# First feed-forward of a fused attention and experts kernel: three PSUM banks for the second product, the sum read out ahead of the weights' conversion, and the first row's conversions two steps later

## The chip, the core and the metric

The kernel runs on one core of a Trainium2 chip. The metric is the device time of one execution in microseconds. Names of engines: PE is TensorE (matmuls; PEld its weight loads), DVE is VectorE, ACT is ScalarE, POOL is GpSimd, SP is SyncE, which issues DMAs. A PSUM bank holds 128 x 512 numbers in fp32, the result of one product here.

## The reference

Three parts stand one behind the other: attention within hash buckets (2 x 8 heads, 768 positions, head size 64), whose output is a matrix x of 1536 x 512; a feed-forward with a rational activation; and a feed-forward of eight experts with a balanced gate. The change touches the second part, and the third takes its output.

```python
def _moe_ref(x, w_in, w_out, a, b):
    h = x @ w_in                                   # x: 1536 x 512, w_in: 512 x 2048
    h2 = h * h
    h3 = h2 * h
    P = a[0] + a[1] * h + a[2] * h2 + a[3] * h3
    Q = 1.0 + np.abs(b[0]) * np.abs(h) + np.abs(b[1]) * h2
    g = P / (Q + 1e-06)
    return (g @ w_out).astype(np.float32)          # w_out: 2048 x 512

def _moe2_ref(x, w_gate, w1, w2):
    P = ...                                        # softmax of x @ w_gate, balanced over 8 rounds
    out = np.zeros((N, D), dtype=np.float32)
    for e in range(E):                             # 8 experts, 512 x 1024 and 1024 x 512 each
        h = np.maximum(x @ w1[e], 0.0)
        out += P[:, e:e + 1] * (h @ w2[e])
    return out
```

The weights `moe_w_in` and `moe_w_out` are given as float64; the kernel is handed their 64-bit patterns and makes fp32 of them on the chip.

## The kernel before

Everything is fp32, and each product is made of three matmuls in a shorter format: every operand is split into a high part (rounded) and a low part (the rest), and high x high, high x low and low x high are added up in PSUM. In the trace, attention takes the time up to about 291 us, the first feed-forward 291 to 616, the experts the rest.

**Steps of the first feed-forward.** The 2048 hidden columns are taken in four rows of 512 (`qf`, NQ = 4), the 1536 tokens in three tiles of 512 (`tt`), and each pair of these in four column blocks of 128 (QF = 4). So there are 4 x 3 x 4 = 48 steps, counted by s in the loop of L633 and after; six more steps at its end belong to the experts. In step s PE makes a first product (`gemm1`, L346, 12 matmuls into a bank `h`), and then, from s = 6 on, a second product (`gemm2_a`, L396, 12 matmuls): for the pair that lies six steps back (QF + ALAG) it multiplies the four activated blocks `gh`, `gl` with one block of 128 columns of w_out, into one PSUM bank. `sum_a` then takes that bank out: in the first row (qf = 0, steps 6 to 17) ACT copies it to `part` (L104), in the later rows DVE adds it to `part` (L407). In the last row (steps 42 to 53) `sum_a` goes on one step later with the split of the result, the operand of the experts' products: x2h on ACT (L104), x2l on DVE (L107, called in L414).

**The banks.** Two tiles of two banks each are in use: `acca`, whose banks take turns for the second product (`j % 2`), and `cvt`, of which the first half is scratch for the conversions and the second half isn't used.

**The activation of a step.** ACT makes three functions of h (L364 to 366), POOL one product (L367), DVE two operations (L368, L369); one step later ACT makes Ln and Exp (L372, L373), DVE three operations (L374 to 376), ACT the copy `gh` (L104) and POOL the rest `gl` (L101).

**The conversions.** While a row is worked on, the eight weight blocks of the next row (four of w_in, four of w_out) are converted, 24 in all. A conversion of one block is: ACT Abs (L165), POOL a limit (L166), DVE four operations on the bits (L176 to 179, with the scratch bank `cvt`), POOL an addition (L182), ACT the high part, POOL the low part. Where it starts is a table (`prep_at`): for w_in at the steps 3, 4, 9, 10 of a row, for w_out at 6, 7, 12, 13. So of any three steps from 3 on, two have a conversion. With the last POOL operations of a block goes the issue of the load of the next raw block (L158, queue of SP).

**What sets the order.** The loop writes the order of PE, ACT, DVE and POOL by hand (a manual schedule). Each of the functions above is a generator that is carried on by `go` piece by piece, and the order in which the loop calls them is the order on each engine. Waits between engines are put in by the framework.

## Time and profile before

| | |
|---|---|
| runs | 1665.7, 1665.38, 1664.59 us; median 1665.38 |
| profiled execution | 1664.14 us, span 1662.4 us |
| PE busy | 1591.3 us (96% of the span) |
| DVE busy | 736.7 us (44%) |
| ACT busy | 563.3 us (34%) |
| POOL busy | 657.3 us (40%) |
| second product of the first feed-forward (L396, acca<-gh) | 384 matmuls, 399 ns each, idle before them 28.9 us, of which 21.7 us end with L407 |
| sum of a bank (L407) | 36 operations, 680 ns each |

The profile shows one execution. A group of it is one line of the kernel on one engine with its tile; "idle before" is the time in which that engine did nothing ahead of these instructions, with the operation that ended it. The span is counted from the first to the last instruction on the core; the execution's own time has a little more at both ends. Operations on DVE overlap at their ends, so the distance from start to start is a little shorter than the duration of one. An idle engine costs time only if it is the one that sets the end.

### The profile page before, as it was taken

Reading aid. Unit: us, or ns where it says so; the run is one execution under the profiler, and the core shown is the slowest. Engines: PE = TensorE matmul, PEld = TensorE weight load, DVE = VectorE, ACT = ScalarE, POOL = GpSimd, SP = SyncE. Lnnn points to the kernel's source line nnn. Section 1 sums busy time; section 2 is a strip of 40 time slices with the busy share of each in tenths; the row PEclk is TensorE's granted clock in tenths of the full one; section 3 lists DMA queues with packets and bytes.
Section 4 is the critical chain, followed back from the end, with each engine's and each line's share of the span. In section 5 each row is a group of like instructions: output and inputs, shape, how many; then the busy total and the mean of one; then the engine's idle time right before and its main releaser. Section 6 shows DMA issues by size and latency. Waiting matters only on the chain.

```text
span 1662.4 us, 19660 instructions
## 1 busy us (share of the span) xinstructions
PE 1591.3 (96%) x7683; PEld 1317.5 (79%) x7683; DVE 736.7 (44%) x1314; ACT 563.3 (34%) x1025; POOL 657.3 (40%) x696
## 2 busy tenths in 40 slices
PE   6999999798888999999999999999999999999998
PEld 5888888576666787888888888888888888888887
DVE  7999999788888742311111111111111111111112
ACT  4887888787676731111111111111111111111110
POOL 7688775677667650150051051042033024015000
PEclk8999999999999999999999999999999999999999
DMA  5232220022111110020020011011012002001001
GB/s 166 80 91 75 73 67 14 26 64 64 51 51 52 38 51 13 14 76 13 1 76 26 0 64 38 1 51 51 1 37 65 0 26 76 1 13 38 1 26 51
DMA packets 49389, 71.67 MB, mean 43 GB/s; under 512 B 4369, under 2 KB 35089, under 8 KB 49297
## 3 DMA queue, kind: packets, MB, share of 16 engines
q1 hardware_dynamic: 49296, 70.42, 14.0%
q8 instruction: 60, 0.98, 0.2%
q14 instruction: 33, 0.26, 0.0%
HBM read 59.79 MB, written 3.15 MB: 38 GB/s over the span
## 4 chain that ended last, share of the span: by engine, by line
PE 74%; DVE 13%; ACT 4%; POOL 4%; issue 3%; DMA 0%; DVEq 0%; POOLq 0%
PE h L346 33%; PE acc L441 31%; PE acca L396 3%; PE av L315 2%; PE pt L300 2%; POOL e L286 1%; DVE tq L374 1%; DVE tu L376 1%; DVE tr L375 1%; DVE e L278 1%; DVE tu L368 1%; DVE ptl L107 1%; DVE cvt L178 1%; DVE cvt L176 1%; DVE part L407 1%
## 5 line engine op out<-in xcount | busy, mean ns | idle before, releaser
L346 PE MATMUL h<-x2h,wa 128*128 128x512 f32 x1536 | 504.7, 390 | 0.0
L427 DVE SCALAR_TENSOR_TENSOR gl<-h,gh 128x512 fp32r<-128x512 f32 x192 | 132.7, 691 | 797.4 <-ACT gh L426 797.4
L441 PE MATMUL acc<-wb,gh 128*128 128x512 f32 x1536 | 474.4, 389 | 0.0
L426 ACT ACTIVATE gh<-h 128x512 fp32r<-128x512 f32 x192 | 114.8, 598 | 894.3 <-PE h L346 894.3
L346 PEld LDWEIGHTS h<-x2h,wa 128*128 128x128 f32 x1536 | 288.5, 188 | 60.1
L441 PEld LDWEIGHTS acc<-wb,gh 128*128 128x128 f32 x1536 | 288.0, 188 | 60.0
L441 PE MATMUL acc<-wb,gl 128*128 128x512 f32 x768 | 298.8, 389 | 0.0
L346 PE MATMUL h<-x2l,wa 128*128 128x512 f32 x768 | 298.8, 389 | 0.0
L98 POOL TENSOR_SCALAR wa<-ra 128x512 fp32r<-128x512 f32 x64 | 40.3, 630 | 533.5 <-PE h L346 533.4
L441 PEld LDWEIGHTS acc<-wb,gl 128*128 128x128 f32 x768 | 144.1, 188 | 29.9
L346 PEld LDWEIGHTS h<-x2l,wa 128*128 128x128 f32 x768 | 144.0, 188 | 29.6
L396 PE MATMUL acca<-gh,wb 128*128 128x512 f32 x384 | 129.8, 399 | 28.9 <-DVE part L407 21.7
L346 PE MATMUL h<-xh,wa 128*128 128x512 f32 x384 | 127.2, 393 | 6.9 <-DVE tu L376 6.9
L396 PEld LDWEIGHTS acca<-gh,wb 128*128 128x128 f32 x384 | 72.2, 188 | 55.2 <-DVE part L407 26.5
L107 DVE TENSOR_TENSOR ptl<-pt,pth 128x512 fp32r<-128x512 f32 x144 | 94.3, 680 | 15.3 <-ACT pth L104 14.5
L286 POOL TENSOR_SCALAR e<-e,rs 128x768 f32<-128x768 f32 x96 | 90.2, 951 | 24.2 <-DVE rs L284 14.6
L279 ACT ACTIVATE e<-e,nm 128x768 f32<-128x768 f32 x96 | 89.8, 935 | 8.5 <-DVE e L278 7.7
L278 DVE TENSOR_SCALAR_CACHE_REDUCE e<-s 128x768 f32<-128x768 f32 x96 | 90.8, 947 | 2.0 <-PE s L271 1.7
L300 PE MATMUL pt<-idr,e 128*128 128x128 f32 x576 | 82.5, 278 | 9.2 <-DVE ptl L107 4.0
L346 PEld LDWEIGHTS h<-xh,wa 128*128 128x128 f32 x384 | 72.5, 189 | 23.6 <-DVE tu L376 8.6
L101 POOL TENSOR_TENSOR wa<-ra,wa 128x512 fp32r<-128x512 f32 x64 | 84.0, 1313 | 5.3
L101 POOL TENSOR_TENSOR wb<-rb,wb 128x512 fp32r<-128x512 f32 x64 | 83.7, 1308 | 5.2
(149 smaller groups left out, 2027.2 us busy)
## 6 DMA issues: line engine op xcount, KB each, us to landing
ra<-in_moe_w_dram SPq DMA_DIRECT2D x32, 512.0 KB
rb<-in_moe_w_dram SPq DMA_DIRECT2D x32, 512.0 KB
ra<-in_moe_w_in_dram SPq DMA_DIRECT2D x16, 512.0 KB
rb<-in_moe_w_out_dram SPq DMA_DIRECT2D x16, 512.0 KB
qkv<-in_q_dram SPq DMA_DIRECT2D x16, 192.0 KB
qkv<-in_k_dram SPq DMA_DIRECT2D x16, 192.0 KB
qkv<-in_v_dram SPq DMA_DIRECT2D x16, 192.0 KB
a<-a SPq DMA_DIRECT2D x16, 192.0 KB
```

The lines of the kernel that those rows point to most:

```text
L98: pool.tensor_scalar(hi, src, 1.0, 0.0, ALU.mult, ALU.add)
L101: pool.tensor_tensor(lo, src, hi.bitcast(F32), ALU.subtract)
L107: dve.tensor_tensor(lo, src, hi.bitcast(F32), ALU.subtract)
L278: dve.tensor_scalar(e[j], s[:, 0:S], BIG, None, ALU.min, ALU.min, accum_out=nm)
L279: act.activation(e[j], e[j], AF.Exp, bias=nm, scale=-1.0, accum_out=rs[:, j:j + 1])
L286: pool.tensor_scalar(e[j], e[j], rs[:, j:j + 1], 0.0, ALU.mult, ALU.add)
L300: pe.transpose(pt[:, c, j * P:(j + 1) * P], e[j][:, cc * P:(cc + 1) * P], idf)
L346: pe.matmul(hps, lhsT=a[:, c], rhs=x[:, c], start=m == 0, stop=m == 3 * KC - 1)
L396: pe.matmul(o, lhsT=l[:, js], rhs=r, start=m == 0, stop=m == 3 * QF - 1)
L426: act.activation(gh, hps, AF.Relu)
L427: dve.scalar_tensor_tensor(gl, hps, 0.0, gh.bitcast(F32), ALU.max, ALU.subtract)
L441: pe.matmul(o, lhsT=l[:, js], rhs=r, start=f == 0 and m == 0, stop=f == EF - 1 and m == 2)
```

## The change

Four things are changed.

- The second product goes to three banks in turn: step s writes bank s mod 3 (n * 4 + j is s - 6). The first two are the two halves of `acca`, the third is the second half of `cvt`, whose first half stays the scratch of the conversions.
- In a step, the sum of the second product (`sum_a`) is called ahead of the DVE operations of a conversion, not behind them.
- The second part of `sum_a` (x2h and x2l, last row) is called near the end of the step that follows, just ahead of that step's sum, not near its beginning.
- The table of the conversions: in the first row w_in starts at the steps 5, 6, 9, 10, not 3, 4, 9, 10, and w_out at 8, 11, 12, 13, not 6, 7, 12, 13. The other rows keep their steps.

```diff
@@ -170,7 +170,7 @@
 
 
         ci = c.bitcast(I32)
-        pc = c if cvt is None else cvt[:, 0]
+        pc = c if cvt is None else cvt
         pi = pc.bitcast(I32)
         low, high = bits[:, :, 0], bits[:, :, 1]
         dve.tensor_scalar(pi, ci, 5, 2, ALU.logical_shift_left, ALU.logical_shift_right)
@@ -386,7 +386,7 @@
 
     def gemm2_a(n, j):
         qf, tt = units[n]
-        o = acca[:, j % 2]
+        o = acca[(n * 4 + j) % 3]
         js = slice(j * P, (j + 1) * P)
         m = 0
         for f in range(QF):
@@ -399,7 +399,7 @@
     def sum_a(n, j):
 
         qf, tt = units[n]
-        o = acca[:, j % 2]
+        o = acca[(n * 4 + j) % 3]
         if qf == 0:
             part[tt, j] = sums.tile([P, 512], F32, tag=f"sum{tt}{j}", name="part")
             act_copy(part[tt, j], o)
@@ -596,6 +596,7 @@
     sums = ffn_pool("sums", 1)
 
     acca, cvt = two_banks("acca"), two_banks("cvt")
+    acca, cvt = (acca[:, 0], acca[:, 1], cvt[:, 1]), cvt[:, 0]
     NU, NS, NB_ = len(units), len(units) * QF, len(steps)
     QS = TT * QF
 
@@ -606,8 +607,8 @@
 
     for qf in range(NQ):
         for j in range(QF):
-            prep_at(qf * QS + (3, 4, 9, 10)[j], 0, (qf + 1) * QF + j)
-            prep_at(qf * QS + (6, 7, 12, 13)[j], 1, (qf + 1) * QF + j)
+            prep_at(qf * QS + ((3, 4) if qf else (5, 6))[j] if j < 2 else qf * QS + 7 + j, 0, (qf + 1) * QF + j)
+            prep_at(qf * QS + ((6, 7) if qf else (8, 11))[j] if j < 2 else qf * QS + 10 + j, 1, (qf + 1) * QF + j)
     for e in range(E):
         for f in range(EF):
             i = FF // P + e * EF + f
@@ -639,7 +640,6 @@
             old_w = narrowing
             narrowing = [prep_weights(m, i) for m, i in preps.get(s, ())]
             narrowing = [w for w in narrowing if go(w)]
-            old_s = [w for w in summing if go(w)]
             for w in old_w:
                 go(w)
             for w in acting:
@@ -652,13 +652,15 @@
                 go(w)
             for w in old_w:
                 go(w), go(w)
-            for w in narrowing:
+            old_s, summing = summing, []
+            for w in old_s:
                 go(w)
-            summing = []
             if 0 <= u < NU:
                 w = sum_a(u, j)
                 if go(w):
                     summing.append(w)
+            for w in narrowing:
+                go(w)
             acting = [new] if n < 0 else []
         assert not (summing and any(go(w) for w in summing)) and not narrowing
 
```

On DVE, a step of a later row that has a conversion, before (L374 to L376 and L368, L369 belong to the activation, L176 to L179 to the conversion, L407 is the sum):

```order
L375 SCALAR_TENSOR_TENSOR tr<-tu,na,tr 128x512
L376 SCALAR_TENSOR_TENSOR tu<-tq,tr 128x512
L368 TENSOR_TENSOR tu<-tu,h 128x512
L369 SCALAR_TENSOR_TENSOR tu<-tu,na,h 128x512
L176 TENSOR_SCALAR cvt<-c 128x512
L177 SCALAR_TENSOR_TENSOR ra<-ra,cvt 128x512
L178 TENSOR_SCALAR cvt<-ra 128x512
L179 SCALAR_TENSOR_TENSOR ra<-ra,cvt 128x512
L407 TENSOR_TENSOR part<-part,acca 128x512
L374 SCALAR_TENSOR_TENSOR tq<-tq,dbias,tr 128x512
```

and after:

```order
L375 SCALAR_TENSOR_TENSOR tr<-tu,na,tr 128x512
L376 SCALAR_TENSOR_TENSOR tu<-tq,tr 128x512
L368 TENSOR_TENSOR tu<-tu,h 128x512
L369 SCALAR_TENSOR_TENSOR tu<-tu,na,h 128x512
L407 TENSOR_TENSOR part<-part,acca 128x512
L176 TENSOR_SCALAR cvt<-c 128x512
L177 SCALAR_TENSOR_TENSOR ra<-ra,cvt 128x512
L178 TENSOR_SCALAR cvt<-ra 128x512
L179 SCALAR_TENSOR_TENSOR ra<-ra,cvt 128x512
L374 SCALAR_TENSOR_TENSOR tq<-tq,dbias,tr 128x512
```

The sum has moved from behind the four operations of the conversion to ahead of them.

On PE, the end of the first product (into `h`) and the beginning of the second product of step 23, with the waits that the program carries (the number behind an engine's name is that of its semaphore), before:

```order
L346 MATMUL h_5623<-xl_99,wa_4944 128x512
L346 MATMUL h_5623<-xh_96,wa_4944 128x512
L396 MATMUL acca_4157<-gh_5138,wb_4398 128x512 [waits DVE_49]
L396 MATMUL acca_4157<-gl_5139,wb_4398 128x512
L396 MATMUL acca_4157<-gh_5138,wb_4398 128x512
```

and after:

```order
L346 MATMUL h_5623<-xl_99,wa_4944 128x512
L346 MATMUL h_5623<-xh_96,wa_4944 128x512
L396 MATMUL cvt_4158<-gh_5138,wb_4490 128x512 [waits DVE_49]
L396 MATMUL cvt_4158<-gl_5139,wb_4490 128x512
L396 MATMUL cvt_4158<-gh_5138,wb_4490 128x512
```

The product writes the tile `cvt` in place of `acca`; there is one wait for DVE in both. The same place in the step behind it, 24, before:

```order
L346 MATMUL h_5673<-xl_99,wa_5215 128x512
L346 MATMUL h_5673<-xh_96,wa_5215 128x512
L396 MATMUL acca_4157<-gh_5349,wb_5054 128x512 [waits DVE_49,Activation_49]
L396 MATMUL acca_4157<-gl_5350,wb_5054 128x512 [waits Pool_49]
L396 MATMUL acca_4157<-gh_5349,wb_5054 128x512
```

and after:

```order
L346 MATMUL h_5673<-xl_99,wa_5215 128x512
L346 MATMUL h_5673<-xh_96,wa_5215 128x512
L396 MATMUL acca_4157<-gh_5349,wb_5054 128x512 [waits Activation_49]
L396 MATMUL acca_4157<-gl_5350,wb_5054 128x512 [waits Pool_49]
L396 MATMUL acca_4157<-gh_5349,wb_5054 128x512
```

Here, where the bank is the first of `acca`, the wait for DVE is gone and that for ACT, which makes `gh`, is left.

On DVE in the last row, from one sum to the next (the tile part_4482 of before is part_4461 of after), before:

```order
L407 TENSOR_TENSOR part_4482<-part_4482,acca_4157 128x512
L107 TENSOR_TENSOR x2l_6378<-part_4482,x2h_6377 128x512
L374 SCALAR_TENSOR_TENSOR tq_6389<-tq_6389,dbias_299,tr_6428 128x512
L375 SCALAR_TENSOR_TENSOR tr_6428<-tu_6387,na_297,tr_6428 128x512
L376 SCALAR_TENSOR_TENSOR tu_6387<-tq_6389,tr_6428 128x512
L368 TENSOR_TENSOR tu_6434<-tu_6434,h_6401 128x512
L369 SCALAR_TENSOR_TENSOR tu_6434<-tu_6434,na_297,h_6401 128x512
L407 TENSOR_TENSOR part_4533<-part_4533,acca_4157 128x512
```

and after:

```order
L407 TENSOR_TENSOR part_4461<-part_4461,acca_4157 128x512
L374 SCALAR_TENSOR_TENSOR tq_6385<-tq_6385,dbias_299,tr_6426 128x512
L375 SCALAR_TENSOR_TENSOR tr_6426<-tu_6383,na_297,tr_6426 128x512
L376 SCALAR_TENSOR_TENSOR tu_6383<-tq_6385,tr_6426 128x512
L368 TENSOR_TENSOR tu_6432<-tu_6432,h_6401 128x512
L369 SCALAR_TENSOR_TENSOR tu_6432<-tu_6432,na_297,h_6401 128x512
L107 TENSOR_TENSOR x2l_6395<-part_4461,x2h_6394 128x512
L407 TENSOR_TENSOR part_4511<-part_4511,cvt_4158 128x512
```

The x2l operation on a sum's result has moved from right behind that sum to just ahead of the next sum; its ACT copy x2h has moved in the same way, from ahead of the next Ln and Exp to behind the next gh.

## Rows read from the trace of the kernel before

**Rows 1.** Windows by stretch: us, busy us (instructions) of each engine, PEclk, DMA share, GB/s.

```profile
320.00:403.00 83.00, 73.96 (x313) 57.85 (x311) 70.87 (x106) 68.41 (x115) 62.22 (x56) 1.00 0.19 58
403.00:531.00 128.00, 109.43 (x466) 86.44 (x467) 114.37 (x172) 87.56 (x142) 87.90 (x78) 1.00 0.17 54
...
616.00:1650.00 1034.00, 1034.00 (x4571) 850.52 (x4570) 206.93 (x346) 116.17 (x195) 224.16 (x235) 1.00 0.10 30
```

**Rows 2.** Waits of PE: who waits for whom, us in total, times, longest.

```profile
PE acca L396 <- DVE part L407: 21.7, 18, 3.0
```

**Rows 3.** Timeline of PE, first matmuls of second products: start, us, what, [idle before <-releaser].

```profile
389.26 0.50 PE L396 MATMUL acca<-gh,wb 128*128 128x512 f32 x1 [0.68 <-ACT part L104]
...
411.02 0.50 PE L396 MATMUL acca<-gh,wb 128*128 128x512 f32 x1 [1.06 <-DVE part L407]
...
423.84 0.50 PE L396 MATMUL acca<-gh,wb 128*128 128x512 f32 x1 [1.64 <-DVE part L407]
...
430.64 0.50 PE L396 MATMUL acca<-gh,wb 128*128 128x512 f32 x1 [1.04 <-DVE part L407]
...
436.21 0.39 PE L396 MATMUL acca<-gh,wb 128*128 128x512 f32 x1
...
528.76 0.50 PE L396 MATMUL acca<-gh,wb 128*128 128x512 f32 x1 [1.07 <-DVE part L407]
```

**Rows 4.** Timeline of DVE, same stretch.

```profile
414.31 0.68 DVE L407 TENSOR_TENSOR part<-part,acca 128x512 f32<-128x512 f32 x1
...
423.11 0.68 DVE L407 TENSOR_TENSOR part<-part,acca 128x512 f32<-128x512 f32 x1
...
429.90 0.68 DVE L407 TENSOR_TENSOR part<-part,acca 128x512 f32<-128x512 f32 x1
...
433.92 0.68 DVE L407 TENSOR_TENSOR part<-part,acca 128x512 f32<-128x512 f32 x1
...
438.56 0.69 DVE L368 TENSOR_TENSOR tu<-tu,h 128x512 f32<-128x512 f32 x1 [0.75 <-ACT tu L366]
...
439.95 0.69 DVE L176 TENSOR_SCALAR cvt<-c 128x512 int32<-128x512 int32 x1
...
442.73 0.68 DVE L407 TENSOR_TENSOR part<-part,acca 128x512 f32<-128x512 f32 x1
...
449.53 0.68 DVE L407 TENSOR_TENSOR part<-part,acca 128x512 f32<-128x512 f32 x1
```

**Rows 5.** Timeline of DVE in the first row: its stall for ACT (first of four).

```profile
343.08 0.75 DVE L374 SCALAR_TENSOR_TENSOR tq<-tq,dbias,tr 128x512 f32<-128x512 f32 x1 [2.14 <-ACT tr L373]
```

**Rows 6.** Timeline of SP (a load of bits), and the window after its landing.

```profile
332.53 6.48 SPq L158 DMA_DIRECT2D rb<-in_moe_w_out_dram  x2
...
335.50:336.00 0.50, 0.50 (x4) 0.41 (x3) 0.50 (x1) 0.47 (x2) 0.50 (x1) 1.00 0.00 0
```

**Rows 7.** Timeline in the last row: PE, then DVE, then ACT, then DVE again.

```profile
561.55 0.49 PE L396 MATMUL acca<-gh,wb 128*128 128x512 f32 x1
...
591.66 0.39 PE L396 MATMUL acca<-gh,wb 128*128 128x512 f32 x1
...
572.95 0.68 DVE L407 TENSOR_TENSOR part<-part,acca 128x512 f32<-128x512 f32 x1
...
573.67 0.63 ACT L104 ACTIVATE x2h<-part 128x512 fp32r<-128x512 f32 x1 [1.34 <-DVE part L407]
...
579.03 0.68 DVE L407 TENSOR_TENSOR part<-part,acca 128x512 f32<-128x512 f32 x1
```

**Rows 8.** Timeline of PE after its two longest waits, and windows behind each.

```profile
315.84 0.50 PE L346 MATMUL h<-xh,wa 128*128 128x512 f32 x1 [3.15 <-DVE tu L376]
...
317.10:320.50 3.40, 3.40 (x10) 2.61 (x9) 3.30 (x6) 3.02 (x5) 2.45 (x3) 0.51 0.28 100
...
404.22 0.50 PE L396 MATMUL acca<-gh,wb 128*128 128x512 f32 x1 [3.01 <-DVE part L407]
...
404.20:410.00 5.80, 5.74 (x24) 4.43 (x24) 5.63 (x9) 2.32 (x5) 4.35 (x4) 1.00 0.26 90
```

## The prediction

> **What bounds the kernel now.** I read the busy time by stretch first, then the waits of TensorE (PE), then the rows of the first feed-forward one by one. By stretch [rows 1], PE is busy for the whole 1034.00 us from 616 to 1650, the second feed-forward: nothing the change does to other engines can gain there. From 320 to 403 PE is idle for 83.00 - 73.96 = 9.0 us and from 403 to 531 for 128.00 - 109.43 = 18.6 us; the reader should see that this first feed-forward is the only place where the edited lines run and PE waits. PE's largest wait of this kernel's second half is that of the second product for the sum L407: 21.7 us in 18 waits [rows 2].
>
> The rows show what that wait is. I number the steps of the first feed-forward s; the second product of step 22 starts at 423.84 and of 23 at 430.64, both just after a sum, and that of 24 at 436.21 without a wait [rows 3]. The product at 423.84 writes the bank whose own sum had started at 414.31, 9.5 us earlier; it started 0.73 us after the sum at 423.11, that of the other bank [rows 4]. So the wait goes by the tile, a pair of banks, and not by the bank. That fact decides most of this case.
>
> What bounds three steps is a loop through VectorE (DVE) and PE: sum 429.90 -> product 430.64 (0.74) -> product 436.21 (5.57) -> L368 at 438.56 (2.35) -> L176 at 439.95 (1.39) -> sum 442.73 (2.78: the four operations of a conversion) -> sum 449.53 (6.80) [rows 3, 4]. Together 19.63 us. Product 20 starts at 411.02 and product 38 at 528.76 [rows 3]: 117.74 us for six such periods, 19.62 each. Matmuls alone would want less: 4571 in 1034.00 us [rows 1] are 0.226 us each, 5.43 us for the 24 of a step, 16.3 us for three.
>
> **The change, part by part. Three banks and sums ahead of conversions, steps 20 to 38.** The third bank is half of the tile whose other half is scratch for the conversions. If waits go by the tile there as well, the product into bank 0 waits for no sum, that into bank 1 for the sum of the step before, which now stands ahead of the conversion, and that into bank 2 (every third step: 20, 23, ... 38) for the last operation of the step before's conversion, since that writes or reads the same tile. Behind the waiting matmul on PE stands the rest of its product and the next step's first product, whose h ScalarE (ACT) needs next, and DVE behind it. So the new loop is: last operation of the conversion to the product 0.75, to the next product 5.57, to L368 2.35, L368 and L369 1.39, sum 0.60, conversion 2.78, then the five activation operations 3.42 (two sums without a conversion between them start 433.92 - 429.90 = 4.02 apart, less 0.60 for the sum), sum 0.60, and 2.18 up to the start of the conversion's last operation (2.78 less 0.60) [rows 4]. The sum is 19.64 us against 19.63. The loop has the same instructions in another order: **0 gained**. What does change is the shape: two waits of 1.64 and 1.04 us [rows 3] become one of about 3.0.
>
> **The first row, up to step 20.** Here the sums are ACT copies and DVE sets the pace: a step with a conversion takes it 3.42 + 2.78 = 6.20 us, one without stalls 2.14 us for ACT [rows 5], so 5.56. The change moves two conversions of each matrix by two to four steps, but leaves as many steps of each kind, so the pace to product 17 stays (389.26 before [rows 3]). At steps 8 and 11 the conversion now also waits for an ACT copy out of bank 2, with L374 of the next step queued behind it on DVE; nearest is DVE's stall of 2.14 for ACT [rows 5], of which I take 0.3 to 0.4 us each, since the copy is a short one that starts earlier: **+0.7**. From product 17 to 20 it took 411.02 - 389.26 = 21.76 us before, because the first sums stood behind conversions; by the new loop it takes 19.6: **-2.2**. Together **-1.4**; bounds 0 (the copies cost what a full stall of 2.14 costs, less the 2.2) and -3 (both hidden). Each moved conversion also moves its ACT and GpSimd operations, and the next load of raw bits on SyncE's queue behind them. That load is issued at 332.53 and by 335.50 nothing moves any more [rows 6]: 3.0 us, where it is wanted a step (5.4 us) or more later. I cost it at 0; without that cover it would be under 1 us of ACT's wait, once.
>
> **The last row's x2h and x2l, steps 44 to 49.** Before, the copy to x2h stands ahead of Ln and Exp on ACT and waits for the sum: sum 572.95, copy 573.67 after a wait of 1.34, next sum at 579.03 [rows 7], 6.08 us for a step in which the matmuls want 5.43. Five steps took 591.66 - 561.55 = 30.11 us [rows 7] against 5 x 5.43 = 27.2. After the change the copy follows gh a step later, when its sum is long done, and x2l stands behind L369; the loop opens and PE is next late for nothing: **-2.9**; bounds -1.5 (half the loop stays through the x2l operation ahead of the sum, some 0.7 us on DVE in each of four steps) and -3.
>
> **The clock.** What the merged waits do to PE's clock is not free. After the wait of 3.15 us before 315.84 the granted clock is 0.51 in 317.10:320.50, that is 1.2 in place of 2.4 GHz, after PE had idled; after the wait of 3.01 us before 404.22 it stays at 1.00 [rows 8]. One drop loses 3.40 x 0.49 = 1.7 us of matmul time. It counts as far as it falls in the 7.9 us (5.57 + 2.35) in which the loop goes through PE; I take 1.4, between 0.9 and 1.7. The waits of about 3 us after the change are nine: before products 11 and 14 and the seven from 20 to 38. (That before product 7, where DVE is late anyway, hides its drop as 317.10 does now.) Of the two nearest rows one dropped, so half of nine: five drops x 1.4 = **+7.0**.
> By the Trainium skill, page "TensorE: Matmul & The Clock Gate", section "HAM oscillation — how this bites in real kernels", waits between batches of matmuls put the clock down again each time, so that every batch pays; the wait before 315.84 agrees, that before 404.22 doesn't. By that rule all nine drop, which is the second rival.
>
> **Sum.** -1.4 + 0 - 2.9 + 7.0 = +2.7 us. The profiled execution took 1664.14 us (its span 1662.4), so 1666.8; it lies 1.2 us under the median of the runs, 1665.38, and on the median the forecast is **1668.1 us**.
>
> **The rivals.** (1) The clock stays up: the merged waits behave like that before 404.22, none or one drops. Then -4.3 to -2.9: 1661.1 to 1662.5. For it: of PE's 18 waits for sums none is followed by a drop. Against it: none but one of those was as long, and that at 315.84, as long, was. (2) Slower: the wait for the conversion puts the clock down nearly every time. The place is each bank-2 product, the price 1.4 us, and it decides from six drops: -4.3 + 6 x 1.4 = +4.1, 1669.5; all nine give +8.3, 1673.7; at 1.7 each, 1676. I take 1671 as its middle. (3) The third bank works as three free banks would: the product waits for its own bank's sum alone, two steps back. Then the loop falls to DVE's work, 3 x 4.02 + 2 x 2.78 = 17.6 us, which is still above PE's 16.3: -2.0 in each of six periods, -12, with no wait long enough for a drop: 1665.4 - 4.3 - 12 = 1649. The rows at 414.31 and 423.84 speak against it, unless the two halves of the scratch tile are told apart.
> By the Trainium skill, page "PSUM — Partial Sum Buffer", section "PSUM bank collisions raise a hardware error", a guard by bank is what the chip needs, so waits by bank would do; the trace shows them by the pair.
>
> **How the numbers follow.** Two to five drops (1663.9 to 1668.1, forecast at the upper end, where half of nine puts it): 0.41. None or one, 1661 to 1662.5: 0.20. Six or more, 1669.5 and up: 0.36. Free banks, 1649: 0.03. A difference of 0.2%, 3.3 us, is about what a measurement of this kernel can tell from none. Faster by more than that (under 1662.1) holds free banks and nearly all of the first rival, 0.22; slower (over 1668.7) the second rival and a little of the forecast's spread, 0.38; within, 0.40. The range leaves out free banks, the lowest of the first rival (the -3 bounds without a drop) and the top of the second (eight or more drops): 1660.5 to 1672.5.
>
> **What would show it.** In the trace after, product 20 should start near 409.6, product 38 near 527.4 plus some 1.4 us for each drop there, the periods being 19.6 us or that plus a drop; the bank-2 products should wait about 3.0 us and be released by L179, no other product for DVE; the tail should run at 5.4 us a step without waits. Stretches of half clock, about 3.4 us long, should follow four to six of the waits. Bank-2 products released by a sum, or periods near 17.6, would make me wrong by 12 us; more waits in the tail, or drops after all waits or none, by 3 to 6.

## The result

The changed kernel takes 1683.96 us (median; 1682.86 to 1684.93) against 1664.99 us for the kernel before in the same runs: a ratio of 1.0114, 95% interval 1.0096 to 1.0131. It is 19 us slower; the forecast was 1668.1, the range ended at 1672.5.

The profiled execution took 1682.86 us, span 1681.1 us against 1662.4. First the stretches of the kernel after, in the columns of [rows 1] (us, busy us of PE, PEld, DVE, ACT, POOL with instructions, PEclk, DMA share, GB/s):

```profile
320.00:403.00 83.00, 69.32 (x273) 55.41 (x273) 67.28 (x100) 62.68 (x105) 59.01 (x54) 0.90 0.21 64
403.00:531.00 128.00, 109.87 (x426) 87.96 (x425) 104.59 (x157) 81.49 (x132) 80.01 (x73) 0.89 0.16 50
531.00:561.00 30.00, 27.00 (x107) 21.74 (x106) 22.65 (x35) 17.44 (x28) 19.14 (x18) 0.89 0.12 36
...
636.00:1660.00 1024.00, 1024.00 (x4526) 842.89 (x4525) 204.11 (x343) 114.55 (x193) 223.01 (x233) 1.00 0.10 30
```

In 128 us from 403 PE is busy for as long as before (109.87 against 109.43 us) and does fewer matmuls in it (426 against 466): the loss isn't in more waiting but in slower matmuls. PEclk tells it: 0.89 and 0.90, where [rows 1] had 1.00.

The waits of PE, as in [rows 2]:

```profile
PE cvt L396 <- DVE rb L179: 16.1, 5, 4.0
PE cvt L396 <- DVE ra L179: 14.7, 5, 3.8
...
PE acca L396 <- ACT part L104: 4.0, 1, 4.0
...
PE acca L396 <- DVE part L407: 0.3, 1, 0.3
```

The 18 waits for sums have become one, and in their place stand ten for L179, the last operation of a conversion, all of them of products into `cvt`: the third bank waits by the tile, as forecast. The products that answer to [rows 3] and [rows 7], here 11, 14, 20, 23, 26, 38, 44 and 49 in the order of time:

```profile
353.82 0.50 PE L396 MATMUL cvt<-gh,wb 128*128 128x512 f32 x1 [3.81 <-DVE ra L179]
...
376.05 0.79 PE L396 MATMUL cvt<-gh,wb 128*128 128x512 f32 x1 [4.01 <-DVE rb L179]
...
416.91 0.77 PE L396 MATMUL cvt<-gh,wb 128*128 128x512 f32 x1 [3.10 <-DVE rb L179]
...
439.26 0.50 PE L396 MATMUL cvt<-gh,wb 128*128 128x512 f32 x1 [3.01 <-DVE ra L179]
...
460.49 0.80 PE L396 MATMUL cvt<-gh,wb 128*128 128x512 f32 x1 [3.01 <-DVE rb L179]
...
546.43 0.79 PE L396 MATMUL cvt<-gh,wb 128*128 128x512 f32 x1 [3.00 <-DVE rb L179]
...
582.02 0.39 PE L396 MATMUL cvt<-gh,wb 128*128 128x512 f32 x1
...
609.96 0.50 PE L396 MATMUL acca<-gh,wb 128*128 128x512 f32 x1 [0.33 <-DVE part L407]
```

Some of the first matmuls behind a wait last 0.8 us and not 0.5: they run at half clock. Windows behind products 20, 23 and 26 of the kernel after, with the full-speed stretch between the first two:

```profile
416.00:422.70 6.70, 5.79 (x14) 4.58 (x15) 4.38 (x8) 3.29 (x6) 5.37 (x5) 0.50 0.25 78
422.80:439.80 17.00, 13.99 (x61) 11.26 (x61) 14.24 (x23) 10.70 (x17) 8.48 (x8) 1.00 0.10 31
439.90:443.20 3.30, 3.30 (x9) 2.57 (x8) 2.66 (x4) 1.92 (x4) 2.87 (x3) 0.50 0.48 138
460.40:463.70 3.30, 3.21 (x8) 2.54 (x9) 3.23 (x6) 1.19 (x3) 2.76 (x3) 0.50 0.31 87
```

So goes every wait of 3 us or more in this trace: with each of the nine that were forecast (3.8 and 4.0 us long in the first row, 3.0 to 3.1 later), and with the 4.0 us ahead of product 7, PE's clock goes to 0.50 for 3.4 or 6.8 us. The tenth wait for L179, 1.82 us ahead of product 17, has no such stretch. The rows give this account of the 18.7 us of span (18.3 of them; the other 0.4 come after product 49):

| stretch | before, us | after, us | moved | forecast |
|---|---|---|---|---|
| start to product 20 | 411.02 | 416.91 | +5.9 | -1.4 and its drops |
| product 20 to 38, six periods | 117.74 | 129.52 | +11.8 | 0 and its drops |
| product 38 to 44 | 32.79 | 35.59 | +2.8 | the drop behind product 38 |
| product 44 to 49 | 30.11 | 27.94 | -2.2 | -2.9 |

### The profile page after: what moved, and what is told of

The parts are those of the page before. It is cut to its first block, busy times and chain, and to the rows that moved or that the text cites. A ratio compares the mean times of both kernels' runs of the same rounds, so it can differ in the third digit from the quotient of the medians.

```text
span 1681.1 us, 19668 instructions
## 1 busy us (share of the span) xinstructions
PE 1606.3 (96%) x7683; PEld 1333.7 (79%) x7683; DVE 738.8 (44%) x1314; ACT 562.7 (33%) x1025; POOL 656.8 (39%) x696
## 4 chain that ended last, share of the span: by engine, by line
PE 79%; DVE 9%; POOL 4%; ACT 4%; issue 2%; DMA 0%; DVEq 0%; SPq 0%; POOLq 0%
PE h L346 35%; PE acc L441 31%; PE cvt L396 3%; PE acca L396 3%; PE av L315 2%; PE pt L300 2%; POOL e L286 1%; DVE e L278 1%; DVE ptl L107 1%; DVE tq L374 1%; DVE tu L376 1%; DVE tr L375 1%; PE s L270 1%; PE s L271 1%; ACT tq L365 1%
## 5 line engine op out<-in xcount | busy, mean ns | idle before, releaser
L396 PE MATMUL acca<-gh,wb 128*128 128x512 f32 x256 | 86.1, 398 | 4.4 <-ACT part L104 4.0
L396 PE MATMUL cvt<-gh,wb 128*128 128x512 f32 x128 | 56.7, 511 | 30.8 <-DVE rb L179 16.1
```

Of the source, the lines that this page charges most:

```text
L396: pe.matmul(o, lhsT=l[:, js], rhs=r, start=m == 0, stop=m == 3 * QF - 1)
```

## The experiments

The runs of four kernels each stood beside runs of the kernel before; every difference below is from the kernel before in the same runs (medians 1664.43, 1664.42 and 1665.23 us) unless another kernel is named, ratios with their 95% intervals. A start read from a trace belongs to one execution. The feed-forward doesn't begin at the same time in each: PE's first wait for L376 ends at 300.88 in the trace of the kernel before and between 299.87 and 302.46 in those of the others. So starts compared across kernels carry 1 to 1.5 us of that; lengths within one trace don't.

**The waits filled.** The half clock is to be taken away and the waits' end left as it is: PE gets work where it would wait. `fill` (its definition is left out here) is twelve matmuls of the step's wa and xh into a bank of its own (`dm`) that nobody reads. Product 8 gets one too, though it doesn't wait in the changed kernel.

```diff
+            if s in (7, 8, 11, 14) or s % 3 == 2 and 20 <= s <= 38:
+                fill(*divmod(s, QF))
             if 0 <= u < NU:
                 gemm2_a(u, j)
```

> The changed kernel with twelve extra matmuls (a repeat of high x high of the first product, into a bank that nobody reads) ahead of the second products of steps 7, 8, 11, 14 and 20, 23 to 38, where PE waits 3 to 4 us for the conversion. The DVE chain that ends the wait is left as it is. Theory A, the clock: the 19 us are lost in the stretches of half clock behind these waits (ten stretches, together 51 us long, in the changed kernel's trace). With 2.7 us of the wait filled the granted clock stays at 1.00, the six periods from product 20 to 38 go from 21.1 to 22.4 us to 19.6, and the time comes to 1660 to 1664 us, 20 us under the changed kernel. Theory B, the waits themselves or the later conversions of the first row set the end and the low clock only follows: the periods stay above 21 us and the time at 1682 or above.

Measured: 1668.27 us, 1.0023 (1.0014 to 1.0033) of before: 15 to 16 us less than the changed kernel, with more work. The clock is 1.00 in the whole feed-forward; the products 20 and 38 (L396 is L403 in this file) and the two windows:

```profile
413.98 0.47 PE L403 MATMUL cvt<-gh,wb 128*128 128x512 f32 x1 [0.38 <-DVE rb L179]
...
531.70 0.50 PE L403 MATMUL cvt<-gh,wb 128*128 128x512 f32 x1 [0.29 <-DVE rb L179]
```

```profile
320.00:403.00 83.00, 76.21 (x331) 61.44 (x330) 69.24 (x103) 64.80 (x108) 60.50 (x55) 1.00 0.21 64
403.00:531.00 128.00, 126.17 (x550) 102.58 (x549) 114.23 (x172) 89.05 (x145) 87.09 (x78) 1.00 0.17 54
```

531.70 - 413.98 = 117.72 us for six periods: 19.62 each, as in the kernel before (19.62) and 0.02 from the sum of the new loop (19.64). So the loop theory holds, and all that the six periods lost is clock. Product 49 stands at 592.39 here and at 609.96 in the changed kernel: between these two traces the clock costs 17.6 us of the 18.7. The profiled execution took 1665.41 us, 2.9 less than the median of its ten runs; by the medians the clock's share is 15 to 16 us, and where the difference lies isn't known. The time didn't come down to 1660 to 1664, though: product 20 is still 3.0 us later than before (411.02), 3.6 counted from the first wait for L376 (300.21 here). That part isn't clock; about 1 us of it may be the fill ahead of product 8 (7 to 8 takes 8.31 us here and 7.21 in the run with two banks, below).

**Every second wait filled.** As above, but of the late waits only those ahead of products 20, 26, 32 and 38.

```diff
-            if s in (7, 8, 11, 14) or s % 3 == 2 and 20 <= s <= 38:
+            if s in (7, 8, 11, 14) or s in (20, 26, 32, 38):
```

> The changed kernel with the extra matmuls ahead of every second of the seven late waits only (products 20, 26, 32, 38; also 7, 8, 11, 14 in the first row). If each wait of 3 us puts the clock down by itself: half clock behind products 23, 29 and 35 alone, the periods that begin with them 21.1 to 22.4 us and the others 19.6, that is 5 to 8 us above the kernel with all waits filled, 1673 to 1676. If it needs several such waits in a row: clock 1.00 throughout and the time of the kernel with all waits filled, 1668.

Measured: 1672.23 us, 1.0046 (1.0029 to 1.0062). Products 23, 26 and 29, and the windows from 403 to 480:

```profile
434.96 0.50 PE L403 MATMUL cvt<-gh,wb 128*128 128x512 f32 x1 [3.00 <-DVE ra L179]
...
456.21 0.50 PE L403 MATMUL cvt<-gh,wb 128*128 128x512 f32 x1 [0.28 <-DVE rb L179]
...
475.82 0.50 PE L403 MATMUL cvt<-gh,wb 128*128 128x512 f32 x1 [3.00 <-DVE ra L179]
```

```profile
403.00:435.70 32.70, 29.33 (x128) 23.65 (x128) 29.79 (x46) 22.74 (x37) 22.04 (x20) 1.00 0.15 49
435.80:439.10 3.30, 3.30 (x9) 2.60 (x8) 2.46 (x4) 2.11 (x4) 2.87 (x4) 0.50 0.51 154
439.20:476.70 37.50, 34.22 (x150) 27.68 (x149) 32.34 (x49) 24.97 (x41) 23.82 (x22) 1.00 0.14 43
476.80:480.10 3.30, 3.30 (x9) 2.52 (x9) 2.32 (x4) 2.25 (x4) 2.87 (x4) 0.50 0.51 158
```

The period with the open wait takes 456.21 - 434.96 = 21.25 us, the one with the filled wait 19.61. Each wait drops the clock by itself, and one such drop costs 1.6 us. Three drops make 5 us; the time is 3 to 4 us above that with all waits filled, a little under the 1673 expected.

**Two banks, the rest as changed.** The edit is made in `gemm2_a` and in `sum_a`.

```diff
-        o = acca[(n * 4 + j) % 3]
+        o = acca[(n * 4 + j) % 2]
```

> The changed kernel with the second product back in two banks in turn (the pair acca), everything else as changed: sums ahead of conversions, first row's conversions later, x2h and x2l later. No product waits for a conversion's last operation any more; it waits for the sum of the step before, which stands ahead of the conversion. If the third bank's tile-wide wait is what costs (mine): periods of three steps fall to DVE's own work, 3 x 4.02 + 2 x 2.78 = 17.6 us, no wait of PE over 2 us in steps 20 to 38, clock 1.00, time 1648 to 1652. If the sum's new place does not help (the loop keeps its length because the product waits for a sum that waits for the product): periods of 19.6, time 1660 to 1663.

Measured: 1659.83 us, 0.9969 (0.9959 to 0.998), 24 us less than with the third bank. Products 20 and 38 start at 411.79 and 524.45: periods of 18.78, not of 17.6. DVE has a stall left, in the step without a conversion:

```profile
436.63 0.68 DVE L407 TENSOR_TENSOR part<-part,acca 128x512 f32<-128x512 f32 x1
438.38 0.75 DVE L374 SCALAR_TENSOR_TENSOR tq<-tq,dbias,tr 128x512 f32<-128x512 f32 x1 [1.07 <-ACT tr L373]
```

The stall of 1.07 for Exp stays; with DVE's work of 17.6 it makes 18.7. (That the period is not held up by this stall alone shows in the runs with Exp earlier, below.) The time of 1648 to 1652 was missed by the first row too (below).

**The scratch in SBUF, so that the third bank shares its tile with nothing.**

```diff
-        pc = c if cvt is None else cvt
+        pc = c
```

> The changed kernel with the conversions' scratch in SBUF (in the tile c itself) and not in the first half of cvt, so that the third bank shares a tile with nothing that DVE writes in a conversion. If the wait goes by the tile: the waits for L179 vanish, three banks in turn are free, periods of 17 to 18 us (DVE's work; the four conversion operations may take other times on SBUF than the 0.69 us each that they take now), time 1645 to 1655. If the bank-2 products wait for something else in the conversion, the waits of 3 us and the low clock stay, time above 1675.

Measured: 1664.68 us, 1.0000 (0.999 to 1.0009). The waits for L179 are gone, which shows that they were the tile's. But products into bank 1 (19, 22, 25 and so on) now wait for sums, by up to 3.68 us for DVE's and 6.21 for an ACT copy in the first row (product 13): banks 0 and 1 are still one tile, and the product into bank 1 waits for the sum of the step before, out of bank 0. Products 23 (into the third bank, without a wait) and 25, and the window behind 25:

```profile
433.58 0.39 PE L396 MATMUL cvt<-gh,wb 128*128 128x512 f32 x1
...
447.02 0.50 PE L396 MATMUL acca<-gh,wb 128*128 128x512 f32 x1 [2.40 <-DVE part L407]
```

```profile
447.90:451.30 3.40, 3.40 (x10) 2.63 (x9) 3.30 (x6) 1.49 (x3) 1.71 (x2) 0.50 0.00 0
```

The periods are 19.0, every second one with half clock in it. DVE and then POOL in the second conversion of a period:

```profile
434.43 0.43 DVE L176 TENSOR_SCALAR c<-c 128x512 int32<-128x512 int32 x1
434.90 1.67 DVE L177 SCALAR_TENSOR_TENSOR ra<-ra,c 128x512 int32<-128x512 int32 x1
436.61 0.43 DVE L178 TENSOR_SCALAR c<-ra 128x512 int32<-128x512 int32 x1
...
434.54 1.48 POOL L101 TENSOR_TENSOR wa<-c,wa 128x512 fp32r<-128x512 f32 x1
```

Two operations became faster (0.43, where they took 0.69 with PSUM), but L177, with both inputs in SBUF, takes 1.67: it is done 0.55 us after the POOL operation that runs beside it ends at 436.02. From the start of L176 to the end of L179 the two conversions of a period take 2.62 and 3.33 us here, 2.86 each with the scratch in PSUM: the faster operations gain nothing.

**The sums back behind the conversions; three banks.**

```diff
-            if 0 <= u < NU:
-                w = sum_a(u, j)
-                if go(w):
-                    summing.append(w)
             for w in narrowing:
                 go(w)
+            if 0 <= u < NU:
+                w = sum_a(u, j)
+                if go(w):
+                    summing.append(w)
```

> The changed kernel with the sums back behind the conversions; three banks, the later conversions and the later x2h stay. If it is the meeting of the two that makes one long wait (the third bank waits for a whole conversion, and the sum ahead of it takes away the other wait that had cut the stall in two): the waits of PE from product 20 on are again two to a period, none over 2 us, the clock stays at 1.00, periods of 19.0 to 19.7 us, time 1660 to 1666. If the third bank alone, by its wait for L179, brings the long waits: periods over 21 us with half clock behind them, time above 1677.

Measured: 1669.77 us, 1.0033 (1.002 to 1.0046). Products 22 and 23, and the windows behind product 11 and from 410:

```profile
437.17 0.50 PE L396 MATMUL acca<-gh,wb 128*128 128x512 f32 x1 [1.64 <-DVE part L407]
...
443.37 0.50 PE L396 MATMUL cvt<-gh,wb 128*128 128x512 f32 x1 [0.45 <-DVE ra L179]
```

```profile
357.00:363.70 6.70, 5.45 (x13) 4.29 (x14) 4.61 (x7) 4.97 (x8) 4.72 (x6) 0.50 0.25 78
410.00:560.00 150.00, 134.98 (x579) 107.17 (x578) 134.43 (x201) 107.60 (x172) 105.64 (x95) 1.00 0.18 53
```

From 410 on two waits stand in a period, the clock is 1.00 and six periods take 114.4 us (product 20 at 424.35, 38 at 538.72), 19.06 each. So the third bank alone doesn't cost in these rows, nor does the early sum alone (its run stands below); they cost together, by making one wait out of two. The time missed its range upwards because of the first row, where the third bank and the later conversions bring two waits of 4.2 us, and half clock behind them. (This trace is of an execution of 1672.34 us, 2.6 over the median.)

**The later conversions alone.** The kernel before with the new table of the first row.

```diff
-            prep_at(qf * QS + (3, 4, 9, 10)[j], 0, (qf + 1) * QF + j)
-            prep_at(qf * QS + (6, 7, 12, 13)[j], 1, (qf + 1) * QF + j)
+            prep_at(qf * QS + ((3, 4) if qf else (5, 6))[j] if j < 2 else qf * QS + 7 + j, 0, (qf + 1) * QF + j)
+            prep_at(qf * QS + ((6, 7) if qf else (8, 11))[j] if j < 2 else qf * QS + 10 + j, 1, (qf + 1) * QF + j)
```

> The kernel before with one part of the change alone: the first row's conversions at the later steps (5, 6, 9, 10 and 8, 11, 12, 13). In the runs with two banks and with the filled waits, product 11 to 14 took 22.28 us where it took 18.06 before: each step from 11 to 13 has a conversion there, and ACT's Abs of the next one waits 1.65 us for GpSimd to be done with the tile c, with Ln and Exp behind it. If that is the first row's loss: 11 to 14 takes 22.3 us here too, product 20 starts 2 to 4 us later than in the kernel before, time 2 to 4 us above it. If the later steps only push work into stalls, as the prediction had it: within 1 us of before.

Measured: 1667.54 us, 1.002 (1.001 to 1.0029): 3 us lost. Product 11 and 14, then 19 with the window behind it:

```profile
350.20 0.50 PE L396 MATMUL acca<-gh,wb 128*128 128x512 f32 x1 [1.68 <-ACT part L104]
...
372.42 0.50 PE L396 MATMUL acca<-gh,wb 128*128 128x512 f32 x1 [1.63 <-ACT part L104]
...
405.46 0.50 PE L396 MATMUL acca<-gh,wb 128*128 128x512 f32 x1 [3.02 <-DVE part L407]
```

```profile
406.90:410.10 3.20, 3.20 (x10) 2.42 (x9) 3.13 (x5) 2.31 (x4) 2.24 (x3) 0.50 0.53 164
```

Product 11 to 14 takes 22.2 us, where it took 353.14 to 371.20, 18.06, in the kernel before. The table also wins something ahead of that: product 6 starts at 315.06 and not 320.05, and product 11 is still 2.9 us earlier than before. Product 20, at 412.67, is 1.65 us later, less than the 2 to 4 expected; counted from the first wait for L376, which ends 1.0 us earlier in this trace, it is 2.7. The steps 11, 12 and 13 each have a conversion, and so had 8 to 10. ACT in such a step (from the run with two banks, which has the same table):

```profile
361.49 0.69 ACT L165 ACTIVATE c<-rb 128x512 f32<-128x512 f32 x1 [1.65 <-POOL wa L101]
362.07 0.68 ACT L372 ACTIVATE tr<-tq,dbias 128x512 f32<-128x512 f32 x1
```

Abs (L165) needs a tile c, of which there are two, and waits for the POOL operation that frees the one of the conversion before the last; Ln stands behind it on ACT, L374 behind Exp on DVE. From the third conversion in a row on, a step takes 7.4 us (10 to 14, 345.06 to 374.76 in that run) and not the 6.2 of DVE's work. DVE, ACT, POOL and PE are each busy for 5.4 to 6.2 us of it, so none of them is full, which points to the chain of waits. Whether a third tile c would lift it wasn't tried.

**The changed kernel with the old table.**

```diff
-            prep_at(qf * QS + ((3, 4) if qf else (5, 6))[j] if j < 2 else qf * QS + 7 + j, 0, (qf + 1) * QF + j)
-            prep_at(qf * QS + ((6, 7) if qf else (8, 11))[j] if j < 2 else qf * QS + 10 + j, 1, (qf + 1) * QF + j)
+            prep_at(qf * QS + (3, 4, 9, 10)[j], 0, (qf + 1) * QF + j)
+            prep_at(qf * QS + (6, 7, 12, 13)[j], 1, (qf + 1) * QF + j)
```

> The changed kernel with the first row's conversions at their old steps; third bank, sum ahead and later x2h stay. By the part measured alone, the later steps cost some 3 us. If the third bank in the scratch's tile is the cause of nearly all of the rest: the waits for L179 then come in the first row at products 8, 11, 14 and 17 too, with half clock behind them, the periods from 20 on stay at 21.1 to 22.4, time 1678 to 1684. If the later steps were what made the waits long enough: no half clock from 320 on, under 1665.

Measured: 1683.46 us, 1.0111 (1.0096 to 1.0126), as the changed kernel. What the old table gives back, the third bank takes in other waits of the first row, products 8 and 11 (14 at 377.80 waits 1.82 us, 17 at 396.27 waits 1.81). The windows behind the first three; behind 17 it is 0.50 again (396.50:399.80):

```profile
337.70 0.50 PE L396 MATMUL cvt<-gh,wb 128*128 128x512 f32 x1 [2.03 <-DVE rb L179]
...
357.76 0.50 PE L396 MATMUL cvt<-gh,wb 128*128 128x512 f32 x1 [1.81 <-DVE ra L179]
```

```profile
338.50:341.80 3.30, 3.30 (x9) 2.56 (x8) 2.51 (x4) 1.15 (x2) 2.87 (x4) 0.50 0.50 155
359.00:362.20 3.20, 3.20 (x9) 2.45 (x9) 2.06 (x4) 1.15 (x2) 2.77 (x3) 0.50 0.56 164
378.00:384.00 6.00, 6.00 (x27) 4.92 (x27) 3.75 (x6) 4.26 (x8) 5.24 (x5) 1.00 0.29 87
```

**x2h and x2l later, alone.** The second part of `sum_a` goes behind gh, where the changed kernel has it.

```diff
-            old_s = [w for w in summing if go(w)]
...
+            old_s, summing = summing, []
+            for w in old_s:
+                go(w)
             for w in narrowing:
                 go(w)
-            summing = []
```

> The kernel before with one part of the change alone: x2h and x2l called a step later, just ahead of the next sum. By the traces of before and after, product 44 to 49 takes 30.11 us before and 27.94 after; expected 27.2 to 28.0 here, time 2 to 3 us under the kernel before (1662 to 1663), clock as before. If the tail's gain is given back behind it (the experts' first product waits for x2h or x2l of the last step), within 0.5 us of before.

Measured: 1663.6 us, 0.9993 (0.9983 to 1.0002). Inconclusive by its time: the interval holds a gain of 2 us and none. Its own trace shows the gain; products 44 and 49:

```profile
562.91 0.50 PE L396 MATMUL acca<-gh,wb 128*128 128x512 f32 x1
...
591.01 0.50 PE L396 MATMUL acca<-gh,wb 128*128 128x512 f32 x1
```

That is 28.10 us where the kernel before takes 30.11, 2.0 gained. The next two runs bear it out: 30.10 without this part, 28.09 with it, and 1.9 us between their times.

**The sum ahead, alone.** The kernel before with the sum called ahead of the conversion.

```diff
+            if 0 <= u < NU:
+                w = sum_a(u, j)
+                if go(w):
+                    summing.append(w)
             for w in narrowing:
                 go(w)
-            if 0 <= u < NU:
-                w = sum_a(u, j)
-                if go(w):
-                    summing.append(w)
```

> The kernel before with one part of the change alone: the sum ahead of the conversion, two banks as before, first row and x2h as before. By the run with two banks the period should be 18.78 us (17.6 of DVE's work and a stall of 1.07 for Exp in the step without a conversion), against 19.62: 5 us in six periods, and 2 us more between product 17 and 20; clock 1.00; time 6 to 8 us under the kernel before. If the sum ahead gains only together with the other parts: within 1 us of before.

Measured: 1658.58 us, 0.9964 (0.9951 to 0.9976): 5.8 us gained, just short of the 6 to 8 expected. With two banks the early sum frees the pair of banks before the conversion begins, and no wait of PE between 403 and 531 is over 1.14 us.

**The two parts that gain.** Two banks, old table, sum ahead, x2h and x2l later: the changed kernel with two edits (the first in both places).

```diff
-        o = acca[(n * 4 + j) % 3]
+        o = acca[(n * 4 + j) % 2]
...
-            prep_at(qf * QS + ((3, 4) if qf else (5, 6))[j] if j < 2 else qf * QS + 7 + j, 0, (qf + 1) * QF + j)
-            prep_at(qf * QS + ((6, 7) if qf else (8, 11))[j] if j < 2 else qf * QS + 10 + j, 1, (qf + 1) * QF + j)
+            prep_at(qf * QS + (3, 4, 9, 10)[j], 0, (qf + 1) * QF + j)
+            prep_at(qf * QS + (6, 7, 12, 13)[j], 1, (qf + 1) * QF + j)
```

> The two parts that gained, without the two that lost: two banks as before, conversions at the old steps, sum ahead of the conversion, x2h and x2l a step later. Sum of the parts: -5 (six periods of 18.78), -2 (product 17 to 20), -2 (last row): 8 to 10 us under the kernel before, 1655 to 1657. If the parts hide one another: at the time of the better of them alone, 6 us under.

Measured: 1656.64 us, 0.9954 (0.9939 to 0.9968): 7.8 us under the kernel before (8 to 10 were expected), 2 us under the sum ahead alone, and 27 us under the changed kernel.

**Exp earlier.** The kernel above with Abs called behind Ln and Exp, and, in a second run, the weight copies of the step before too (all lines from `for w in later` on, which the first run doesn't have).

```diff
-            narrowing = [prep_weights(m, i) for m, i in preps.get(s, ())]
-            narrowing = [w for w in narrowing if go(w)]
             for w in old_w:
                 go(w)
             for w in acting:
                 go(w)
+            narrowing = [prep_weights(m, i) for m, i in preps.get(s, ())]
+            narrowing = [w for w in narrowing if go(w)]
+            for w in later:
+                go(w), go(w)
...
-            for w in old_w:
-                go(w), go(w)
+            later = old_w
```

> The best kernel so far (two banks, old steps, sum ahead, x2h later) with Abs of a conversion (ACT) and its limit (GpSimd) called behind Ln and Exp, not ahead of them. In the trace with two banks DVE stalls 1.07 us a period for Exp, and between the activation's last DVE operation and Exp stand gh, a weight copy (0.53) and Abs (0.57) on ACT. If that chain is what keeps the period at 18.78 and not at DVE's 17.6: about 0.5 less a period and as much in each of the first row's stalls of 2.14, together 4 to 6 us under the best so far, 1651 to 1653. If the wait only goes elsewhere (the conversion waits for its later limit): within 1 us of it.

> The same with the weight copy (ACT) and its low part (GpSimd) also behind Ln and Exp, in the step after. If ACT's chain is the limit: the stall goes to nearly none, periods of 17.6 to 17.9, 7 to 10 us under the best so far, 1647 to 1650. If GpSimd's later low part now delays its product L367, on which Ln waits: no faster than the one without this step.

Measured: 1656.0 us, 0.9946 (0.9931 to 0.9961), with Abs moved, and 1666.33 us, 1.0006 (0.9997 to 1.0016), with the copies as well. The first is within noise of the kernel above: products 20 and 38 start at 408.97 and 521.13, 18.69 a period in place of 18.79. DVE in the step without a conversion:

```profile
453.62 0.75 DVE L374 SCALAR_TENSOR_TENSOR tq<-tq,dbias,tr 128x512 f32<-128x512 f32 x1 [0.51 <-ACT tr L373]
...
456.13 0.69 DVE L368 TENSOR_TENSOR tu<-tu,h 128x512 f32<-128x512 f32 x1 [0.38 <-ACT tu L366]
```

The stall for Exp did shrink by half, from 1.07 to 0.51, as expected; but DVE now waits 0.38 us for ACT's function of h (L366), and h comes from PE. So Abs set half of the stall, and the stall wasn't what alone set the period. The second is worse, 19.8 a period (412.93 to 531.62); that the low part, which stands ahead of L367 on GpSimd there, is the reason was expected and fits, but wasn't tried by itself.

## Why the prediction was wrong

**The loop: right.** Steps 20 to 38 were to gain nothing, with one wait of about 3.0 us in place of two, released by L179. The rows show 3.00 to 3.10 us, and with the clock held up by filled waits the period is 19.62.

**How often the clock drops: wrong, and this failed the forecast first of all.** The step "of the two nearest rows one dropped, so half of nine" took two rows for a rate. All nine dropped. The second rival, "all nine", had the right mechanism. By the Trainium skill, page "TensorE: Matmul & The Clock Gate", section "HAM oscillation — how this bites in real kernels", waits between batches of matmuls, of about 3 to 5 us in its example, put the clock down at every batch; the trace of the changed kernel agrees, nine of nine at 3.0 to 4.0 us, and the single row at 404.22 [rows 8] that spoke against it weighed too much. Of that row the later runs say that it goes either way: the same wait ahead of product 19 did drop the clock in the kernel with the later conversions (3.02 us, window 406.90:410.10 above) and didn't in the kernel with x2h later alone (2.97 us, 1.00 in 402.50:412.00). Nor are the seven late waits seven independent trials: the six periods below repeat after three. Two other kernels with the same loop say the same, though: seven of seven with the old table, three of three open waits with every second one filled.

**What a drop costs: too small.** 1.4 was taken, between 0.9 and 1.7. The six periods of the changed kernel are 22.35, 21.23, 21.14, 22.40, 21.24 and 21.16 us long; less 19.62 that is 1.5 to 1.6 for a stretch of 3.4 us and 2.7 to 2.8 for one of 6.8. The long kind wasn't thought of, and so the second rival's 1673.7, or 1676 at 1.7 each, also falls short. By the traces with and without filled waits the clock makes 17.6 us, where 7.0 stood in the sum: four drops too few at 1.4 are 5.6 of the difference, the price, 2.0 and not 1.4 for each of nine, is 5.0.

**The first row: wrong in sign.** Forecast -1.4 (the bound of -3 that it names for "both hidden" doesn't follow: with both copies at nothing, -2.2 is left); without any clock loss product 20 came 3.0 us later. Two steps failed. "Leaves as many steps of each kind, so the pace to product 17 stays" looked at DVE alone. It counted the conversions and not how closely they follow one another: from the third in a row on ACT's Abs waits for GpSimd to free one of the two tiles c, and product 11 to 14 takes 22.2 to 22.3 us instead of 18.06. And 0.7 for the third bank was too little: in the changed kernel products 11 and 14 wait 3.8 and 4.0 us for L179. With filled waits and the clock up product 17 starts at 394.26, with two banks and the same table at 392.82, though that trace's feed-forward begins 2.0 us later (300.21 and 302.17): 3.4 us, of which the fill ahead of product 8 may be 1. The last part of the term, 19.6 from product 17 to 20, held: 394.26 to 413.98 with filled waits, 19.7.

**The last row: mechanism right, size a little off.** -2.2 for -2.9; one wait of 0.33 for a sum is left ahead of product 49; the bound of -1.5 had allowed for waits of that kind.

**Free banks: a rival that wasn't run as such.** Three banks in three tiles of their own weren't tried: with the scratch in SBUF the first two still share a tile. Its 17.6 us a period left out DVE's stall of 1.07 for Exp; measured is 18.78 with two banks and the sum ahead. Its idea, that the sum ahead of the conversion takes the wait away where it isn't tied to the scratch, is what the best kernels here do. I tied it to three banks and didn't see that two are enough.

With the measured terms the sum is +3.0 (first row) + 0 - 2.2 + 17.6 (clock) = 18.4 us, against 18.7 of span. The terms are differences between the same three traces, so that the sum comes out is bookkeeping; it shows where the 18.7 us lie, 15.7 more than the +2.7 forecast: 10.6 of the clock, 4.4 of the first row, 0.7 of the last.

## What to carry to other kernels

Before a change that moves waits, add up what each wait will be afterwards: two short waits of an engine that end in the same time as one long one are not the same thing on TensorE, since here each of the six such waits from product 20 to 35 cost 1.5 to 2.8 us of half clock on top. A bank that shares a tile with somebody's scratch is not a free bank; look at what releases the whole tile. When a step's load is moved, count not only how many such steps there are but how many follow one another, and look at the buffers that they pass through.

## What the runs showed of the hardware

A wait of the same length doesn't always do the same: waits of 1.81 us ahead of product 11 (357.76) and 1.82 ahead of product 14 (377.80) of the kernel with the old table differ, the first with half clock behind it and the second with 1.00 (378.00:384.00 above), and the wait of 3.0 us ahead of product 19 dropped the clock in one kernel and not in the kernel before, nor in the one with x2h later alone. Shorter waits can do it as well: with the scratch in SBUF the three of 2.36 to 2.40 us ahead of products 25, 31 and 37 each have half clock behind them (447.90:451.30 above). What decides it these runs leave open. How long a stretch lasts goes, in the changed kernel, with where it begins: the five of 6.8 us begin 0.8 us or more before the wait ends (416.00:422.70 is at 0.50 from its start, product 20 starts at 416.91), the five of 3.4 us begin behind its end or at most 0.2 us before it (439.90:443.20, product 23 at 439.26).

A DVE operation with both inputs in SBUF waited for a GpSimd operation to end (L177 in the kernel with the scratch in SBUF: 1.67 us, where it takes 0.69 with one input in PSUM). L179 of that kernel, with both inputs in SBUF too, takes 0.69 with no GpSimd operation beside it (437.07) and 0.98 beside L166 (348.68). By the Trainium skill, page "SBUF — State Buffer", section "SBUF: two separate sides", such an operation and a GpSimd one that reads SBUF exclude one another for the whole instruction; the trace agrees.
